# Which PSUM bank pairs w_in's tiles take: the third and the seventh tile, and the order of pairs in the third batch

## The chip, the cores and the metric

The kernel runs on one core of a Trainium2 chip. A core has five engines with queues of their own: TensorE (PE; its weight loads are listed as PEld), VectorE (DVE), ScalarE (ACT), GpSimd (POOL) and SyncE (SP, which issues DMAs). TensorE writes its results to PSUM, which has eight banks here, each of 128 partitions by 512 float32; this kernel uses all eight. The metric is device time in microseconds, the median of several runs.

## What is computed

Cosine attention over 8 batches, 12 heads, 448 rows of 64 elements, followed by a feed-forward layer with an exact GELU:

```python
q_n = q / (np.linalg.norm(q, axis=-1, keepdims=True) + 1e-06)
k_n = k / (np.linalg.norm(k, axis=-1, keepdims=True) + 1e-06)
scores = np.matmul(q_n, k_n.transpose(0, 1, 3, 2)) / tau
attn = np.exp(scores - np.max(scores, axis=-1, keepdims=True))
attn = attn / (np.sum(attn, axis=-1, keepdims=True) + 1e-09)
attn_out = np.matmul(attn, v)                 # (8, 12, 448, 64)
x = attn_out.transpose(0, 2, 1, 3).reshape(3584, 768)
h = x @ w_in                                  # (3584, 2048)
g = 0.5 * h * (1.0 + erf(h / sqrt(2)))
return g @ w_out                              # (3584, 768)
```

## The kernel before

Batches run one after another, b = 0 to 7. The twelve heads of a batch form NQ = 3 groups of four; group g0 = 3b is a batch's first. The order of all instructions is written out by hand, and each engine works through its own in that order, waiting where a result or a buffer is not there yet.

**Attention.** For each group, q and k are loaded (SyncE), squared (GpSimd, L159), reduced (VectorE, L168), turned into inverse norms, scaled to bf16 (GpSimd, L204) and transposed by DMA (L216). Then come seven score passes per group, one for each chunk c of 64 keys for the group's four heads: `scores` (L242) issues four matmuls into a pair of PSUM banks, and `exps` (L252) has ScalarE write exp of both banks to SBUF as bf16. `visit(b, pairs)` (L637) runs the next passes of batch b, one for each number in `pairs`; the number says which bank pair the pass takes. A pass can write its pair only when the exponential of the pair's last pass has been read out. The sums of the exponentials come either from TensorE (`sums`, L311) or, for a batch's third group, from GpSimd (`folded`, L264). `values` (L325) multiplies them with v into a bank pair, too, and `normalise` (L359) has VectorE multiply the result with the inverse sums; that product is two of the six row blocks of x. `weighted(g, p)` is values and normalise of group g in pair p.

**Feed-forward.** `first(b)` multiplies x of batch b with w_in: 16 tiles (m = 0 to 15) of 128 rows of the hidden layer by 448 columns, each six matmuls (L800; KD = 6 row blocks of x), and GELU by ScalarE (L853) into g. The second product, with w_out, is cut into pieces of 16 matmuls (`second_pieces`, L396), which are run as filling between the score passes of the next batch: `run()` takes the next number of them.

**The banks.** Three pairs of two banks, 0, 1 and 2, serve score passes, values and some tiles of w_in. Two single banks, `mm_tile`, alternate between the other tiles of w_in, the sums and the w_out pieces. In `first`, `pairs` (L795) says which tiles take a pair: an entry m: p gives tiles m and m + 1 the two banks of pair p. All other tiles take the single banks in turn. For b of 2 and more, tiles 0 to 5 come first, in the order 0, 2, 3, 4, 5, 1, with the first four row blocks of x each; then the fifth row block of all six, then the sixth; then tiles 6, 7, 8 and so on, each complete. The fifth and sixth row blocks of x are the product of the batch's third group, which is the last thing that VectorE makes of attention.

**What stands around the change.** For b = 3 to 6 the score passes that stand directly ahead of `first(b)` belong to batch b + 1:

```python
visit(b + 1, (1, 2))
weighted(g0 + 2, 0)
visit(b + 1, (1,))
```

Then `first(b)` starts with its tiles. For b = 2 the end of attention is the part that the diff shows, and `visit(b + 1, (1, 2))` and `weighted(g0 + 2, 0)` are its last steps. For b = 7 no passes of a next batch exist, and the last step is `both(g0 + 2, 0)`, sums and values of the third group in pair 0; the last score pass, in pair 2, stands ahead of 22 matmuls with w_out. The next batch's attention starts with filling and then takes pairs 1 and 2 for two passes and pair 0 for values.

Of the kernel before, what the change touches and what calls it, by code (L numbers as in the profile page):

```python
# [16 lines left out]
def kernel(  # L17
# [154 lines left out]
    def logs(n):  # L172
        nq = nq_t.pop(n)
        ln_t[n] = nrm.tile(list(nq.shape), F32, tag="lq", name=f"lq{n}")
        nc.scalar.activation(ln_t[n], nq, AF.Ln, bias=tiny)

    def roots(n):
        ln = ln_t.pop(n)
        sr_t[n] = root2[2 if len(groups[n]) == 2 else n % 2][:, :math.prod(shapes[n])]
        nc.scalar.activation(sr_t[n][:, :, 0], ln.rearrange("p j i s c -> p (j i s c)"), AF.Exp, scale=0.5)  # L180

    def inverses(n):
        sr = sr_t.pop(n)
        shape = [128] + shapes[n]
        se = nrm.tile(shape, F32, tag="se", name=f"se{n}")
        nc.vector.tensor_reduce(se.rearrange("p j i s c -> p (j i s c)"), sr, mybir.AxisListType.X, ALU.add)  # L186
        rn = nrm.tile(shape, F32, tag="rn", name=f"rn{n}")
        nc.vector.reciprocal(rn, se)  # L188
        rn_t[n] = rn
# [42 lines left out]
    def scores(g, banks, p=None):  # L232
        qkT = qkT_t[g]
        if p is None:
            p = st_turn[0]
            st_turn[0] ^= 1
        st = pair(p, f"st{g}_{banks[0][1]}")
        for n, (s, c) in enumerate(banks):
            rows = slice(64 * s, 64 * (s + 1))
            for h in range(2):  # L240
                cols = slice(64 * h, 64 * (h + 1))
                nc.tensor.matmul(st[cols, n, :S], lhsT=qkT[rows, 1, c, cols], rhs=qkT[rows, 0, :, cols],  # L242
                                 start=True, stop=True, tile_position=(64 * s, 64 * h))
        st_t[g, banks[0]] = st

    def exps(g, banks):
        st = st_t.pop((g, banks[0]))
        if g not in all_t:
            all_t[g] = ptp.tile([128, C, 2, S], BF16, tag="pt", name=f"pt{g}")
        (s0, c0), (s1, c1) = banks  # L250
        pt = all_t[g][:, c0] if c0 == c1 else all_t[g][:, c0:c1 + 1, s0]
        nc.scalar.activation(pt, st[:, :, :S], AF.Exp, scale=inv_tau)  # L252
        for n, (s, c) in enumerate(banks):
            pt_t[g, s, c] = pt[:, n]
# [106 lines left out]
    def total(g):  # L361
        sums(g)
        turned(g)
        inverted(g)
        spread(g, 0)
        spread(g, 1)

    def weighted(g, p):
        values(g, p=p)
        for h in range(2):  # L370
            if (g, h) not in rs_t:
                spread(g, h)
            normalise(g, h)

    def both(g, p):
        total(g)
        weighted(g, p)
# [66 lines left out]
    def upto(f, n, last=None):  # L444
        last = {load_qk: NG, load_v: NV, root: len(groups), load_wi: NQ + 1, load_wo: 4}.get(f, NU)
        while done.get(f, 0) < min(n, last):
            done[f] = done.get(f, 0) + 1
            f(done[f] - 1)
# [188 lines left out]
    def visit(b, pairs):  # L637
        for p in pairs:
            n, c = passes[at.get(b, 0)]
            at[b] = at.get(b, 0) + 1  # L640
            scores(b * NQ + n, ((0, c), (1, c)), p)
            exps(b * NQ + n, ((0, c), (1, c)))

    def attention(b, fill):
        fill = list(fill)
        if b == 1:
            parts = iter((20, 13, 14, 17, 16, 16))
        elif b == 2:
            parts = iter((20, 16, 16, 16, 16, 14, 14, 15, 1))
        elif b == B - 1:  # L650
            parts = iter((14, 14, 14, 14, 18, 22))
        elif len(fill) == 128:
            parts = iter((20, 18, 18, 18, 14, 24, 4, 6, 6))
        else:
            parts = iter((14, 12, 12, 12, 14, 16, 4, 6, 6))

        def run(n=None):
            for _ in range(next(parts) if n is None else n):
                fill.pop(0)()

        x_t[b] = xp.tile([128, KD, S], BF16, tag="x", name=f"x{b}")
        g0, u = b * NQ, b * NQ + 1
        run()
        upto(scale, u + 3)
        if b == 2:
            upto(load_qk, g0 + NQ + 3)
        upto(transposes, u + 3)
        if b == 1:
            upto(load_qk, g0 + NQ + 2)
            upto(square, u + 4)  # L670
            visit(b, (0, 1, 2))
            run()
            visit(b, (0, 1, 2))
            run()
            upto(load_qk, g0 + NQ + 3)
            visit(b, (0, 1))
            upto(square, u + 5)
            run()
            visit(b, (0, 1, 2))
            both(g0, 0)  # L680
            upto(load_v, b + 3)
            upto(load_qk, g0 + NQ + 4)
            visit(b, (1, 2))
            upto(reduce, u + 4)
            run()
            visit(b, (1, 2, 0))
            both(g0 + 1, 1)
            visit(b, (2, 0))
            logs(6)
            roots(6)  # L690
            run()
            both(g0 + 2, 2)
            inverses(6)
            done[root] = 7
            return
        upto(scale, u + 4)
        if b == 2:
            upto(load_qk, g0 + NQ + 4)
        upto(transposes, u + 4)
        n = 2 * b + 5  # L700

        def norms():
            if n < len(groups):
                logs(n)
                roots(n)
                inverses(n)
                done[root] = n + 1

        if b == 2:
            visit(b, (0, 1, 2))  # L710
            run()
            upto(load_qk, g0 + NQ + 5)
            upto(square, u + 6)
            visit(b, (0, 1, 2))
            run()
            visit(b, (1, 2))
            total(g0)
            weighted(g0, 0)
            upto(load_v, b + 3)
            visit(b, (1, 2))  # L720
            upto(reduce, u + 5)
            run()
            visit(b, (0, 1, 2))
            folded(g0 + 2, range(2))
            run()
            visit(b, (1, 2))
            total(g0 + 1)
            weighted(g0 + 1, 0)
            visit(b, (1, 2))
            folded(g0 + 2, range(2, C - 1))  # L730
            run()
            upto(reduce, u + 6)
            visit(b, (0,))
            folded(g0 + 2, range(C - 1, C))
            visit(b + 1, (1, 2))
            norms()
            run()
            visit(b + 1, (0, 1, 2))
            run()
            turned_all(g0 + 2)  # L740
            run()
            inverted_all(g0 + 2)
            visit(b + 1, (1, 2))
            weighted(g0 + 2, 0)
        else:
            visit(b, (1, 2))
            weighted(g0, 0)
            visit(b, (1,))
            run()
            upto(load_qk, g0 + NQ + 4)  # L750
            visit(b, (2, 0, 1))
            upto(reduce, u + 5)
            run()
            upto(reduce, u + 6)
            visit(b, (2, 0, 1))
            run()
            upto(load_qk, g0 + NQ + 5)
            visit(b, (2, 0))
            total(g0 + 1)
            if b + 1 < B:  # L760
                folded(g0 + 2, range(4))
            weighted(g0 + 1, 1)
            visit(b, (2, 0))
            if b + 1 < B:
                folded(g0 + 2, range(4, C - 1))
            norms()
            run()
            visit(b, (2,))
            if b + 1 < B:
                folded(g0 + 2, range(C - 1, C))  # L770
                upto(load_v, b + 3)
                visit(b + 1, (0, 1))
                run()
                turned_all(g0 + 2)
                run()
                visit(b + 1, (2, 0))
                run()
                inverted_all(g0 + 2)
                run()
# [3 lines that stand above are left out]
            else:  # L783
                run()
                both(g0 + 2, 0)
        assert not fill, len(fill)

    def first(b):
# [3 lines left out]
        nc.scalar.preload_act_table_set(GELU_SET)  # L792
        u = (b + 1) * NQ + 1
        hps = {}
        pairs = ({0: 1, 2: 0, 6: 1, 8: 0}, {2: 0, 4: 1, 6: 2, 8: 0}, {2: 1, 4: 2})[min(b, 2)]  # L795
        ahead = 6 if b else 5

        def mm(m, kds):
# [134 lines left out]
```

## Time and profile before

| | us |
|---|---|
| median of 3 runs | 409.73 (409.33 to 409.84) |
| the profiled execution | 409.18 |
| its span, first to last instruction | 407.4 |

| engine | busy us | share of the span |
|---|---|---|
| ScalarE | 247.2 | 61% |
| GpSimd | 250.0 | 61% |
| VectorE | 239.1 | 59% |

A line of a group view gives the source line, the engine, the operation, the tile written and those read, the shape and the count, then busy time and the mean of one in ns, then the engine's idle time just before and what ended it:

```text
L800 PE MATMUL hp<-x,wi 128*128 128x448 bf16 x768 | 148.5, 352 | 0.8 <-ACT pt L252 0.6
L853 ACT ACTIVATE g<-hp 128x448 bf16<-128x448 f32 x128 | 64.1, 552 | 76.4 <-PE hp L800 75.9
L252 ACT ACTIVATE pt<-st 128x896 bf16<-128x896 f32 x168 | 143.0, 916 | 54.1 <-PE st L242 53.9
L359 DVE TENSOR_TENSOR x<-o,rs 128x448 bf16<-128x448 f32 x48 | 27.9, 610 | 14.2 <-PE o L325 13.2
```

Matmuls overlap: the mean of 352 ns is the length of one from start to its modelled end, and the next starts before that. A line of the timeline gives start and length in us, engine, line, operation, tiles, shape and count, and in brackets the idle time before it with what ended it; instructions that follow each other without a break are merged into one line.

### The profile page before, as it was taken

The page shows a single profiled execution, that of the slowest core. Times are in us where ns is not written, and L with a number is a line of the kernel's source. Part 1 is how long each engine was busy: PE and PEld are TensorE (multiplying, and loading weights), DVE is VectorE, ACT ScalarE, POOL GpSimd, SP SyncE. Part 2 cuts the span into 40 slices and gives each one's busy share as a digit, 9 for nine tenths or more (in the row PEclk, how much of TensorE's full clock was granted, in tenths as well). Part 3 has the DMA queues.
Part 4 walks back from the last instruction along what each step waited for, and adds up shares of the span by engine and source line. Part 5 has one row for each costly group of instructions (what it writes and reads, how often), then busy time and mean ns, then how long its engine had stood idle before and what let it go on. Part 6 is the DMA issues. An engine that isn't in the chain of part 4 may idle for free.

```text
span 407.4 us, 8074 instructions
## 1 busy us (share of the span) xinstructions
PE 400.3 (98%) x3343; PEld 207.7 (51%) x3343; DVE 239.1 (59%) x438; ACT 247.2 (61%) x360; POOL 250.0 (61%) x160
## 2 busy tenths in 40 slices
PE   7999999999999999999999999999999999999996
PEld 3445545555554555555555555545555455455564
DVE  5787215951477966587656975668655981360021
ACT  6995695577767458655566557855656555724300
POOL 5899606084899983999739994799919940000000
PEclk9999999999999999999999999999999999999999
DMA  8999999745494905577173932769032830130033
GB/s 293 260 257 214 204 230 324 155 117 155 109 263 86 216 5 127 181 142 146 29 221 99 213 73 34 237 114 208 0 89 60 158 55 2 39 79 2 0 79 77
DMA packets 66484, 54.52 MB, mean 134 GB/s; under 512 B 38672, under 2 KB 62352, under 8 KB 66448
## 3 DMA queue, kind: packets, MB, share of 16 engines
q1 hardware_dynamic: 54464, 41.79, 40.0%
q0 software_dynamic: 11600, 11.80, 18.1%
q8 instruction: 26, 0.43, 0.4%
q10 hardware_dynamic: 384, 0.43, 0.4%
q14 instruction: 10, 0.08, 0.1%
HBM read 45.61 MB, written 11.01 MB: 139 GB/s over the span
## 4 chain that ended last, share of the span: by engine, by line
PE 87%; ACT 3%; DMA 3%; DVE 3%; POOL 2%; issue 1%; POOLq 0%
PE op L396 34%; PE hp L800 31%; PE st L242 9%; PE o L325 6%; DMA qkT<-qkb 3%; ACT pt L252 3%; PE sm L311 2%; PE spin L453 2%; POOL qkb L204 1%; PE op L415 1%; PE sm L302 1%; POOL sq L159 1%; PE tp L221 1%; DVE nq L168 1%; DVE tr L333 0%
## 5 line engine op out<-in xcount | busy, mean ns | idle before, releaser
L252 ACT ACTIVATE pt<-st 128x896 bf16<-128x896 f32 x168 | 143.0, 916 | 54.1 <-PE st L242 53.9
L800 PE MATMUL hp<-x,wi 128*128 128x448 bf16 x768 | 148.5, 352 | 0.8 <-ACT pt L252 0.6
L396 PE MATMUL op<-wo,g 128*128 128x384 bf16 x864 | 148.9, 327 | 0.0
L396 PEld LDWEIGHTS <-g 128*128 128x128 bf16 x864 | 81.0, 98 | 64.7 <-issue 14.1
L800 PEld LDWEIGHTS <-wi 128*128 128x128 bf16 x768 | 74.4, 98 | 73.9 <-issue 6.2
L853 ACT ACTIVATE g<-hp 128x448 bf16<-128x448 f32 x128 | 64.1, 552 | 76.4 <-PE hp L800 75.9
L204 POOL TENSOR_TENSOR qkb<-qk,rn 128x896 bf16<-128x896 f32 (+1 forms) x50 | 80.1, 1629 | 29.4 <-DVE rn L188 29.2
L400 DVE COPY ot<-op 128x384 f32<-128x384 f32 x54 | 29.3, 542 | 79.0 <-PE op L396 77.0
L264 POOL TENSOR_TENSOR acc<-acc,pt 128x896 f32<-128x896 f32 (+1 forms) x50 | 73.0, 1460 | 4.2 <-ACT pt L252 0.5
L159 POOL TENSOR_TENSOR sq<-qk 128x1792 f32<-128x1792 f32 (+1 forms) x22 | 66.5, 3038 | 13.7 <-DMA qk<-in_k_dram 13.7
L168 DVE TENSOR_REDUCE nq<-sq 128x28 f32<-128x1792 f32 (+2 forms) x30 | 48.6, 1633 | 10.1 <-POOL sq L159 7.3
L242 PE MATMUL st<-qkT 64*64 64x448 bf16 x672 | 49.5, 358 | 0.7 <-DVE x L359 0.3
L325 PE MATMUL o<-pt,v 64*64 64x448 bf16 x672 | 37.0, 351 | 0.0
L359 DVE TENSOR_TENSOR x<-o,rs 128x448 bf16<-128x448 f32 x48 | 27.9, 610 | 14.2 <-PE o L325 13.2
L264 POOL TENSOR_TENSOR acc<-pt 128x896 f32<-128x896 bf16 (+1 forms) x10 | 14.5, 1453 | 28.6 <-ACT pt L252 28.6
L242 PEld LDWEIGHTS <-qkT 64*64 64x64 bf16 x672 | 16.7, 105 | 24.7 <-issue 17.8
L354 DVE STREAM_TRANSPOSE rs<-rc 128x448 f32<-128x448 f32 x48 | 28.6, 625 | 0.7
L268 DVE TENSOR_REDUCE acc<-pt 128x448 f32<-128x3136 bf16 x5 | 28.1, 5619 | 0.0
L325 PEld LDWEIGHTS <-v 64*64 64x64 bf16 x672 | 18.6, 107 | 14.4 <-issue 4.4
L273 DVE STREAM_TRANSPOSE ta<-acc 128x896 f32<-128x896 f32 x10 | 11.1, 1112 | 17.6 <-POOL acc L264 17.6
L333 DVE STREAM_TRANSPOSE tr<-sm 128x448 f32<-128x448 f32 x14 | 9.1, 648 | 15.1 <-PE sm L311 12.8
L186 DVE TENSOR_REDUCE se<-root 128x28 f32<-128x56 f32 (+2 forms) x18 | 4.0, 221 | 17.9 <-ACT root L180 17.8
(48 smaller groups left out, 170.7 us busy)
## 6 DMA issues: line engine op xcount, KB each, us to landing
qk<-in_q_dram SPq DMA_DIRECT2D x23, 448.0 KB, 5.4
qk<-in_k_dram SPq DMA_DIRECT2D x23, 448.0 KB, 6.0
out_dram<-ot SPq DMA_DIRECT2D x48, 192.0 KB, 3.0
v<-in_v_dram POOLq DMA_DIRECT2D x7, 672.0 KB, 6.8
wo<-in_moe_w_out_dram POOLq DMA_DIRECT2D x4, 768.0 KB, 13.5
wi<-in_moe_w_in_dram POOLq DMA_DIRECT2D x4, 512.0 KB, 14.5
out_dram<-ot SPq DMA_DIRECT2D x12, 96.0 KB, 2.2
wi<-in_moe_w_in_dram POOLq DMA_DIRECT2D x4, 256.0 KB, 13.9
```

What stands on the lines that cost most here:

```text
L159: eng.tensor_tensor(sq[:, part], t[:, part], t[:, part], ALU.mult)
L168: nc.vector.tensor_reduce(nq[:, part], sq[:, part], mybir.AxisListType.X, ALU.add)
L204: eng.tensor_tensor(qkb[:, i, :, s0:s1].rearrange("p c s d -> p s c d"), t[:, i, s0:s1], rn[:, i].to_broadcast([128, s1 - s0, C, D]), ALU. ...
L242: nc.tensor.matmul(st[cols, n, :S], lhsT=qkT[rows, 1, c, cols], rhs=qkT[rows, 0, :, cols], start=True, stop=True, tile_position=(64 * s, 6 ...
L252: nc.scalar.activation(pt, st[:, :, :S], AF.Exp, scale=inv_tau)
L264: nc.gpsimd.tensor_tensor(to, all_t[g][:, 0, s] if c == 1 else to, all_t[g][:, c, s], ALU.add)
L325: nc.tensor.matmul(bank_t[g, h][cols, :S], lhsT=v_t[g][rows, s, c, :], rhs=pt_t[g, s, c][rows], start=(c == 0), stop=(c == C - 1), tile_po ...
L354: nc.vector.transpose(rs, bank_t[g, "rc"][:, h].to_broadcast([128, NB, 32]))
L396: nc.tensor.matmul(ps[:, :NH], lhsT=g_t[sb][:, kf, t * 128:(t + 1) * 128], rhs=wo[:, kf, ni * NH:(ni + 1) * NH], start=(kf == 0), stop=(kf ...
L400: nc.vector.tensor_copy(ot[:, ni * NH:(ni + 1) * NH], ps[:, :NH])
L800: nc.tensor.matmul(hps[m], lhsT=wi[:, kd, m * 128:(m + 1) * 128], rhs=x_t[b][:, kd, :], start=(kd == 0), stop=(kd == KD - 1))
L853: nc.scalar.activation(g_t[sb][:, m, hf * S:(hf + 1) * S], hps.pop(m), AF.Gelu)
```

## The change

It changes which bank pair three things take, and nothing else: the same instructions stand in the same order on each engine, with other PSUM addresses and so other waits.

In `first`, for b = 2 to 7, tiles 2 and 3 move from pair 1 to pair 2, tiles 4 and 5 from pair 2 to pair 1, and tiles 6 and 7 from the two single banks to pair 0. Tile 8 then takes the single bank that tile 0 had, and tile 9 that of tile 1. In the third batch (b = 2) the last passes take the pairs in another order, so that the pass after the second group's values does not take pair 0.

```diff
             run()
             upto(reduce, u + 6)
-            visit(b, (0,))
+            visit(b, (1,))
             folded(g0 + 2, range(C - 1, C))
-            visit(b + 1, (1, 2))
+            visit(b + 1, (2, 0))
             norms()
             run()
-            visit(b + 1, (0, 1, 2))
+            visit(b + 1, (1, 2, 0))
             run()
             turned_all(g0 + 2)
             run()
...
-        pairs = ({0: 1, 2: 0, 6: 1, 8: 0}, {2: 0, 4: 1, 6: 2, 8: 0}, {2: 1, 4: 2})[min(b, 2)]
+        pairs = ({0: 1, 2: 0, 6: 1, 8: 0}, {2: 0, 4: 1, 6: 2, 8: 0}, {2: 2, 4: 1, 6: 0})[min(b, 2)]
```

## The prediction

> **What bounds the kernel now.** I read the page first (busy shares, granted clock), then the waits of TensorE, then the chain of waits through one batch, then the weight loads in order of time. b is the batch number and tile m a 128-row tile of w_in's output, both counted from 0 as in the code: the third tile is tile 2, the seventh tile 6.
>
> From the page, and from the waits of TensorE over the whole span:
>
> ```profile
> PE 400.3 (98%) x3343; PEld 207.7 (51%) x3343; DVE 239.1 (59%) x438; ACT 247.2 (61%) x360; POOL 250.0 (61%) x160
> PEclk9999999999999999999999999999999999999999
> ...
> PE hp L800 <- ACT pt L252: 0.6, 4, 0.2
> PE st L242 <- DVE x L359: 0.3, 1, 0.3
> ```
>
> TensorE is the bound: 98% busy at full clock, the others near 60%. Its waits look tiny, 0.6 us in four places at w_in's matmuls (L800) and 0.3 us in one at the scores (L242), but these idle times are counted from modelled ends of matmuls. So I go by starts. The chain through the end of b = 3's attention (pieces: start, length, what):
>
> ```profile
> 172.08 2.06 PE op L396 x12
> 174.13 0.34 PE st L242 x4
> 174.50 2.63 ACT pt L252 x3
> 177.17 8.48 PE hp L800 x44
> 185.69 9.24 PE hp L800 x48
> ```
>
> The chain leaves TensorE for 2.63 us, for three exponentials in a row, and comes back to the third tile of w_in. The same piece stands at 224.43, 269.16 and 319.09 us (b = 4, 5, 6), and between 124 and 383 us the chain leaves TensorE nowhere else, but for pieces of issue of 0.04 us or less. It holds no DMA and no GpSimd there. Now the weight loads, one ahead of each matmul (start, length, count, and in brackets the idle time before):
>
> ```profile
> 123.37 0.33 PEld L242 LDWEIGHTS <-qkT 64*64 64x64 bf16 x12 [0.66 <-DVE x L359]
> ...
> 126.44 0.33 PEld L242 LDWEIGHTS <-qkT 64*64 64x64 bf16 x12 [0.32 <-issue]
> ...
> 131.66 9.01 PEld L800 LDWEIGHTS <-wi 128*128 128x128 bf16 x49 [0.36 <-issue]
> 140.96 8.80 PEld L800 LDWEIGHTS <-wi 128*128 128x128 bf16 x47 [0.29 <-issue]
> ...
> 176.08 0.68 PEld L800 LDWEIGHTS <-wi 128*128 128x128 bf16 x5 [0.36 <-issue]
> 177.17 8.23 PEld L800 LDWEIGHTS <-wi 128*128 128x128 bf16 x44 [0.41 <-issue]
> 185.69 8.80 PEld L800 LDWEIGHTS <-wi 128*128 128x128 bf16 x47 [0.29 <-issue]
> ```
>
> In an undisturbed run of loads each takes 0.098 us and the step is (8.80 - 0.10)/46 = 0.189 us, so 0.09 us of idle between two is normal. Three holes are larger. (1) After the fifth load, 0.41 us: four matmuls belong to tile 0, the fifth load is ahead for tile 2, and its matmul is held. The hole is in b = 3 to 6 and not in b = 2 or 7, where the 49 loads are one piece. (2) After the 49th load, 0.29 us, in b = 2 to 7 alike: 48 matmuls make eight tiles, and tile 8's first one is held. It starts with the next load, at 140.96, 185.69, 235.62, 280.35, 330.28 and 373.92. (3) Before the scores at 123.37, 0.66 us where 0.32 is usual. What ends them is seen on the other engines (ScalarE's and VectorE's rows in order of time):
>
> ```profile
> 123.24 0.54 DVE L400 COPY ot<-op 128x384 f32<-128x384 f32 x1
> ...
> 130.27 1.73 ACT L252 ACTIVATE pt<-st 128x896 bf16<-128x896 f32 x2 [0.86 <-PE st L242]
> 137.74 3.76 ACT L853 ACTIVATE g<-hp 128x448 bf16<-128x448 f32 x8 [4.44 <-PE hp L800]
> 142.29 0.54 ACT L853 ACTIVATE g<-hp 128x448 bf16<-128x448 f32 x1 [0.79 <-PE hp L800]
> ...
> 177.14 1.28 ACT L792 ACT_TABLE_LOAD   x1
> ...
> 179.28 0.62 DVE L359 TENSOR_TENSOR x<-o,rs 128x448 bf16<-128x448 f32 x1
> ...
> 180.49 0.62 DVE L359 TENSOR_TENSOR x<-o,rs 128x448 bf16<-128x448 f32 x1
> 181.03 5.60 DVE L268 TENSOR_REDUCE acc<-pt 128x448 f32<-128x3136 bf16 x1
> ```
>
> **The change part by part.** No instruction is added or removed; only PSUM banks change, and with them what a tile waits for.
>
> *The third tile, b = 3 to 6.* Score passes end in the order pair 2, values in pair 0, pair 1. Before, tile 2 takes pair 1, the last pass, whose exponential ends as the table load begins, 177.14. After, it takes pair 2, whose exponential ends one pass earlier: the three fill 174.50 to 177.12, some 0.86 us each, so near 176.25. Without a wait tile 2 starts four steps after 176.08, at 176.85, so the wait is gone. Tile 4 now needs the last pass, but stands eight more steps on, at 178.36, 1.2 us after it. Saved: 0.41 - 0.09 = 0.32 by the hole; from the pieces, b = 3 takes 177.17 + 8.23 - 176.08 = 9.32 us for 49 loads and b = 2 takes 9.01, so 0.31. I take 0.31, four times: 1.24 us. Lower bound: the profile's own 0.6 us.
>
> *The seventh and eighth tiles, b = 2 to 7.* Before, tiles 0, 1, 6, 7, 8 ... alternate on two single banks, so tile 8 takes the bank of tile 6 and waits for its GELU. Eight GELUs fill 137.74 to 141.50, and the last, tile 7's, starts when its matmuls end, so tile 6's ends just before 140.96, where tile 8 starts. After, tiles 6 and 7 have pair 0, and tile 8 takes tile 0's bank, free since some 138.3 us. Saved: 0.29 - 0.09 = 0.20 us, six times: 1.20 us. The lower bound is 0, if the hole is the issue that the bracket names. The next use of the single banks, tile 10 after tile 8, has spare: the GELU that starts at 142.29 ends at 142.83 and tile 10 would start two tiles after 140.96, at 143.23, 0.4 us later. Both move together, so nothing is late there. Without this cover all would be given back at tile 10.
>
> *Pair 0 for tile 6.* It held the last values, which VectorE turns into x (L359), ended at 181.11. The last of the six row blocks of x is that same product, and the matmuls with it stand ahead of tile 6, so TensorE has waited already: 0 us. Its next user, the first values of the next batch, comes near 153 us for b = 2; tile 7's GELU ends by 141.5, 11 us before.
>
> *The third batch (b = 2).* The order of pairs changes from 0 | 1, 2 | 0, 1, 2 | 1, 2 to 1 | 2, 0 | 1, 2, 0 | 1, 2. The pass at 123.37 used pair 0 and waited for VectorE's product of the values there, whose chain ends at 123.32. Now it takes pair 1, whose exponential ended two passes back, and pair 0 comes third. It starts 0.66 - 0.32 = 0.34 us earlier, at 123.03; the third pass stands 0.4 us behind (twelve matmuls busy 0.76 us, one 0.35), at 123.43, after 123.32. Saved 0.34 us, lower bound 0. Tile 2 of b = 2 now takes pair 2, the last pass: its exponential ends at 132.00 and the tile starts four steps after 131.66, at 132.42, 0.4 us later. Both move together: 0 us.
>
> *Who must now be earlier.* x of the last head group: after the third tile's wait is gone, its two row blocks are needed at 180.62 and 181.75 (24 and 30 steps after 176.08); VectorE's rows end at 179.90 and 181.11. 0.7 us is left, and GpSimd's sums that feed it start with exponentials, so they move too. GpSimd idles 28.9 us in six places between 120 and 383 us waiting for exponentials, so it keeps up.
>
> The sum: 1.24 + 1.20 + 0.34 = 2.78 us of the profiled execution's 409.18 us (span 407.4), which stands 0.55 us below the median of 409.73. I take it off the median: **406.95 us**. With all lower bounds 0.6 us is saved.
>
> The waits view counts 0.9 us for holes that I put at 1.58. The Trainium skill (Perfetto Trace Analysis, Per-engine timelines, Tensor Engine Instruction) says a matmul's reported end is computed from its size, not observed. By it the waits view can't price these holes, and the starts can; by the waits view alone the sum would be 0.9 us, 408.8.
>
> The clock row is 9 in all slices, so the holes cost no clock here. The Trainium skill (TensorE: Matmul & The Clock Gate, A second HAM failure mode) tells of a kernel whose small PSUM stalls made the clock fall; by that rule closing them would give more than 2.8 us, by the row it doesn't.
>
> **The rivals.**
> *A: the hole at tile 8 is issue, as its bracket says.* For: the name. Against: it is always at the one place where two banks are short, and ScalarE is busy without a break until then. Saved 1.24 + 0.34: 408.15. 8%.
> *B: the time is hidden anyway,* a supplier off TensorE ends batches at the same instant. For: x has only 0.7 us of spare. Against: no DMA or GpSimd piece in the chain after 124 us. 409.7. 4%.
> *C: slower.* Tile 6 waits for pair 0 beyond the product, until VectorE's next instruction, the 5.60 us reduction, has ended (b = 2 to 6). In b = 3 that is 186.63 against a start at 182.90: 3.7 us, five times, less 2.8: 425.4. It decides from 0.56 us a batch. For: only that VectorE works in order. Against: the same product releases the matmuls with x while that reduction runs. 2%.
> *D: a part fails,* such as the third batch's 0.34 us or two of the third tiles: 407.3 to 407.9. 6%.
>
> **How the numbers follow.** The forecast has 80%, with its own range 406.4 to 407.5 from the spread of the runs before. A and D lie up to 408.2, so 406.2 to 408.2 holds well over 8 in 10. All lower bounds at once (409.1) would need three separate causes, and I leave that out. What can be told from no change is 0.2%, 0.8 us. Faster: the forecast, A and D, 94%; same: B, 4%; slower: C, 2%.
>
> **What would show it.** In the profile after: no wait of hp L800 for pt L252; the 2.63 us pieces of ScalarE gone from the chain; 96 loads of L800 in one piece, with no 0.41 or 0.29 before any; 0.32 instead of 0.66 near 123 us. A hole that moves to tile 10, or one at tile 6, would prove me wrong, as would an unchanged 0.29 at tile 8.

## The result, and the profile after

| | before | after |
|---|---|---|
| median us (6 runs each) | 409.78 | 407.03 |
| range | 409.33 to 410.82 | 406.79 to 407.22 |
| profiled execution, its span | 409.18, 407.4 | 407.06, 405.3 |

The ratio is 0.9928, with a 95% interval of 0.9915 to 0.9941: 2.75 us less by the medians, clear of no change. The forecast was 406.95 us (2.78 us less). Here and below, medians and ratios leave out the executions that ran some 6 us longer at a granted clock of 0.976 to 0.984, which several of the kernels had.

The page's busy line and clock row of the changed kernel, and below them the waits of TensorE over the whole span:

```profile
PE 398.9 (98%) x3343; PEld 207.9 (51%) x3343; DVE 239.0 (59%) x438; ACT 247.3 (61%) x360; POOL 250.0 (62%) x160
PEclk9999999999999999999999999999999999999999
...
PE spin L453 <- DVE root L91: 1.9, 1, 1.9
PE st L242 <- DMA qkT<-qkb: 0.6, 1, 0.6
PE st L242 <- ACT pt L252: 0.2, 1, 0.2
```

The busy share is 98% before and after, so it could not have told of this change. The waits of hp L800 for pt L252 and of st L242 for x L359 are gone. What is left is start-up and one wait for a DMA transpose near 59 us, before the first changed instruction.

The chain of waits through the end of b = 3 (start, length, what):

```profile
172.19 2.06 PE op L396 x12
174.25 0.50 PE st L242 x8
174.75 1.32 PE o L325 x28
176.08 0.19 PE st L242 x4
176.27 18.27 PE hp L800 x96
```

The 2.63 us piece of ScalarE is out of the chain, and all 96 matmuls of w_in are one piece. In order of time the weight loads say the same:

```profile
123.68 0.45 PEld L242 LDWEIGHTS <-qkT 64*64 64x64 bf16 x12 [0.32 <-issue]
...
131.97 17.90 PEld L800 LDWEIGHTS <-wi 128*128 128x128 bf16 x96 [0.36 <-issue]
...
176.19 17.90 PEld L800 LDWEIGHTS <-wi 128*128 128x128 bf16 x96 [0.36 <-issue]
```

The brackets of 0.41 and 0.29 us are gone from these two batches and from b = 4 to 7, and the 0.66 near 123 us is the usual 0.32. (These twelve loads take 0.45 and not 0.33 us, because the last four come late: they start at 124.02, just after VectorE's product of the second group ends at 123.96. The four matmuls with them start at 124.08, at their usual distance, so nothing is lost.)

The profiled spans differ by 2.1 us only. The rest was lost before the change begins. The DMA wait near 59 us in the two profiled executions, before and after:

```profile
58.50 0.57 PE L242 MATMUL st<-qkT 64*64 64x448 bf16 x8 [0.26 <-DMA qkT<-qkb]
```

```profile
59.16 0.57 PE L242 MATMUL st<-qkT 64*64 64x448 bf16 x8 [0.62 <-DMA qkT<-qkb]
```

After it this execution of the changed kernel is 0.66 us late: 0.36 us from this wait, and 0.30 us because two more of the warm-up matmuls at its start (L453) ran at 0.37 us a step in place of 0.19. Comparing the start of each matmul with its counterpart, it then gains 0.34 us at the third batch's scores, 0.32 at each of four third tiles and 0.19 to 0.20 at each of six ninth tiles: 0.34 + 4 x 0.32 + 6 x 0.196 = 2.8 us. It gains and loses nothing anywhere else after 60 us.

### The profile page after: what moved, and what is told of

Its sections match the earlier page's. It is cut to its first block, busy times and chain, and to the rows that moved or that the text cites. A ratio compares the mean times of both kernels' runs of the same rounds, so it can differ in the third digit from the quotient of the medians.

```text
span 405.3 us, 8074 instructions
## 1 busy us (share of the span) xinstructions
PE 398.9 (98%) x3343; PEld 207.9 (51%) x3343; DVE 239.0 (59%) x438; ACT 247.3 (61%) x360; POOL 250.0 (62%) x160
## 4 chain that ended last, share of the span: by engine, by line
PE 91%; DMA 3%; POOL 2%; DVE 2%; issue 1%; ACT 0%; POOLq 0%
PE op L396 34%; PE hp L800 32%; PE st L242 10%; PE o L325 8%; DMA qkT<-qkb 3%; PE spin L453 2%; PE sm L311 2%; PE op L415 1%; POOL qkb L204 1%; PE sm L302 1%; POOL sq L159 1%; PE tp L221 1%; DVE nq L168 1%; DVE rn L188 0%; ACT pt L252 0%
## 5 line engine op out<-in xcount | busy, mean ns | idle before, releaser
L252 ACT ACTIVATE pt<-st 128x896 bf16<-128x896 f32 x168 | 143.1, 916 | 54.0 <-PE st L242 53.7
L800 PE MATMUL hp<-x,wi 128*128 128x448 bf16 x768 | 146.9, 353 | 0.0
L800 PEld LDWEIGHTS <-wi 128*128 128x128 bf16 x768 | 74.4, 98 | 71.4 <-issue 2.9
L242 PE MATMUL st<-qkT 64*64 64x448 bf16 x672 | 49.5, 358 | 0.8 <-DMA qkT<-qkb 0.6
L359 DVE TENSOR_TENSOR x<-o,rs 128x448 bf16<-128x448 f32 x48 | 28.0, 610 | 13.7 <-PE o L325 12.7
L242 PEld LDWEIGHTS <-qkT 64*64 64x64 bf16 x672 | 16.8, 105 | 24.7 <-issue 18.1
```

The source lines that it names most:

```text
L800: nc.tensor.matmul(hps[m], lhsT=wi[:, kd, m * 128:(m + 1) * 128], rhs=x_t[b][:, kd, :], start=(kd == 0), stop=(kd == KD - 1))
```

## The experiments

In all of them the pairs are those of b = 2 to 7. The diffs of the first three are against the kernel before, the others against the changed kernel; `...` marks what is left out. For each, "starts" means that the start of each matmul of its profiled execution is compared with that of the same matmul in the kernel named.

**The third tile alone**

```diff
-        pairs = (..., {2: 1, 4: 2})[min(b, 2)]
+        pairs = (..., {2: 2, 4: 1})[min(b, 2)]
```

> Only tiles 2 to 5 change pairs (b = 2 to 7); tiles 6 and 7 stay in the single banks and the third batch keeps its old order of pairs. My theory: the hole after the fifth load of w_in goes in b = 3 to 6 (0.32 us each), the hole after the 49th load (0.20 us, b = 2 to 7) and the 0.66 us ahead of the scores near 123 us stay: 1.27 us less than before, about 408.5 us. Rival (the parts hide each other: an earlier third tile only makes tile 8 wait longer for its GELU): the hole after the 49th load grows by what the first one loses and the time stays at 409.7.

Measured: 408.58 us, ratio 0.9982 (0.9964 to 1.0001); the interval just touches no change, widened by one execution of 412.89 us among twelve, so here the profile decides. Starts against the kernel before: 0.32 us gained at the third tile of b = 3, 4, 5 and 6 and nothing else after 60 us. Its weight loads in b = 3:

```profile
176.42 9.01 PEld L800 LDWEIGHTS <-wi 128*128 128x128 bf16 x49 [0.36 <-issue]
185.72 8.80 PEld L800 LDWEIGHTS <-wi 128*128 128x128 bf16 x47 [0.29 <-issue]
```

The first hole is gone (49 loads in one piece of 9.01 us), the second is still 0.29 us. It did not grow, so the rival falls: the two holes do not hide each other.

**The seventh tile alone**

```diff
-        pairs = (..., {2: 1, 4: 2})[min(b, 2)]
+        pairs = (..., {2: 1, 4: 2, 6: 0})[min(b, 2)]
```

> Only tiles 6 and 7 take pair 0 (b = 2 to 7); tiles 2 to 5 and the third batch are as before. My theory: the hole after the 49th load goes in six batches (0.20 us each), the 0.41 us after the fifth load stays in b = 3 to 6: 1.18 us less than before, about 408.6 us. Rival (that hole is instruction issue, as the bracket in the profile names it): it stays at 0.29 us and the time is 409.7.

Measured: 408.60 us, ratio 0.9974 (0.9961 to 0.9986). Starts against the kernel before: 0.196 to 0.198 us gained in each of six batches. Weight loads in b = 3:

```profile
176.66 0.68 PEld L800 LDWEIGHTS <-wi 128*128 128x128 bf16 x5 [0.36 <-issue]
177.75 17.12 PEld L800 LDWEIGHTS <-wi 128*128 128x128 bf16 x91 [0.41 <-issue]
```

Now it is the other way round: the 0.41 stays, the 0.29 is gone. The bracket called the hole issue; the change of a bank closed it. So it was a wait for the bank, whatever the bracket says. In the kernel before, the GELU of tile 6 in b = 2 and the first matmul of tile 8 stand like this:

```profile
140.31 0.60 ACT L853 ACTIVATE g<-hp 128x448 bf16<-128x448 f32 x1
140.96 0.35 PE L800 MATMUL hp<-x,wi 128*128 128x448 bf16 x1
```

The GELU ends at 140.91, and the matmul starts 0.05 us later.

**The third batch's order alone**

```diff
+            visit(b, (1,))
...
+            visit(b + 1, (2, 0))
...
+            visit(b + 1, (1, 2, 0))
...
         pairs = (..., {2: 1, 4: 2})[min(b, 2)]
```

> Only the order of pairs in the third batch changes. My theory: 0.32 us of idle instead of 0.66 ahead of the scores near 123 us, all other holes as before: 0.34 us less, about 409.4 us, hardly to be told by the median but by the profile. Rival (the pass in pair 0, now third, waits instead): a hole of about 0.3 us between the second and third pass and no gain.

Measured: 409.22 us, ratio 0.9988 (0.9980 to 0.9997). Starts against the kernel before: 0.341 us gained at the first pass after the second group's values, nothing else changes after 60 us. The weight loads of that pass and the two behind it:

```profile
123.20 0.45 PEld L242 LDWEIGHTS <-qkT 64*64 64x64 bf16 x12 [0.32 <-issue]
```

The pass in pair 0, now third, does not delay its matmuls.

**The changed tiles with the old order of the third batch**

```diff
-            visit(b, (1,))
+            visit(b, (0,))
...
-            visit(b + 1, (2, 0))
+            visit(b + 1, (1, 2))
...
-            visit(b + 1, (1, 2, 0))
+            visit(b + 1, (0, 1, 2))
```

> The changed pairs of w_in's tiles with the old order of pairs in the third batch. My theory: 0.66 us of idle is back near 123 us and nothing else: 0.34 us above the changed kernel, about 407.4 us; the order of pairs is not needed for the tiles' gain. Rival (tile 2 in b = 2 now takes the pair of the last pass and needs the new order): a hole after the fifth load of b = 2 and 0.3 us more than that.

Measured: 407.41 us, ratio 0.9956 (0.9933 to 0.9979); one execution of 412.61 us among eleven pulls the ratio up, and by the medians it is 2.3 us less than before. Starts against the changed kernel: 0.341 us lost at that pass, nothing else after 60 us. Its weight loads:

```profile
123.82 0.33 PEld L242 LDWEIGHTS <-qkT 64*64 64x64 bf16 x12 [0.66 <-DVE x L359]
...
132.12 17.90 PEld L800 LDWEIGHTS <-wi 128*128 128x128 bf16 x96 [0.36 <-issue]
```

The 0.66 is back and the 96 loads of b = 2 are whole, so tile 2 does not need the new order. The parts add up: by the medians 1.0 + 1.0 + 0.4 = 2.4 us for the three alone, by starts 1.28 + 1.18 + 0.34 = 2.8. The medians of single parts are no better than a few tenths of a microsecond.

**Pair 0 for tiles 8 and 9 in place of 6 and 7**

```diff
-        pairs = (..., {2: 2, 4: 1, 6: 0})[min(b, 2)]
+        pairs = (..., {2: 2, 4: 1, 8: 0})[min(b, 2)]
```

> As the changed kernel, but pair 0 goes to tiles 8 and 9 in place of 6 and 7. My theory: the hole came from tile 8 waiting for tile 6's GELU, and any bank that spares tile 8 this wait does as well: tiles 6 and 7 take the banks of tiles 0 and 1 and tile 10 that of tile 6, long free. No hole in the 96 loads, time equal to the changed kernel, about 407.0 us. Rival (what helps is that tiles 6 and 7 leave the single banks, so that their start waits for no GELU): a hole of about 0.2 us after the 37th or the 49th load in six batches, 408.2 us.

Measured: 406.71 us, ratio 0.9933 (0.9921 to 0.9944), like the changed kernel. From 60 us on, its starts differ from the changed kernel's by no step. Weight loads in b = 3:

```profile
176.55 17.90 PEld L800 LDWEIGHTS <-wi 128*128 128x128 bf16 x96 [0.36 <-issue]
```

So tiles 6 and 7 can stay in the single banks: it is enough that tile 8 needs another bank than tile 6's.

**Pair 0 for tiles 10 and 11**

```diff
-        pairs = (..., {2: 2, 4: 1, 6: 0})[min(b, 2)]
+        pairs = (..., {2: 2, 4: 1, 10: 0})[min(b, 2)]
```

> As the changed kernel, but pair 0 goes to tiles 10 and 11 in place of 6 and 7. My theory: tile 8 has to wait for tile 6's GELU again, so the 0.29 us hole after the 49th load is back in all six batches, and the time is 1.18 us above the changed kernel, about 408.2 us. Rival (two more banks anywhere in the stage give the slack): no hole, 407.0 us.

Measured: 408.49 us, ratio 0.9969 (0.9956 to 0.9982). Starts against the changed kernel: 0.197 us lost at tile 8 in each of six batches. Weight loads in b = 3:

```profile
177.09 9.01 PEld L800 LDWEIGHTS <-wi 128*128 128x128 bf16 x49 [0.36 <-issue]
186.38 8.80 PEld L800 LDWEIGHTS <-wi 128*128 128x128 bf16 x47 [0.29 <-issue]
```

So two more banks help only if tile 8 is spared tile 6's GELU. These two runs and the seventh tile alone settle what the hole was. The 0.3 us beyond the expected 408.2 is not this hole: in the profiled execution (408.92 us) 0.7 us was lost against the changed kernel in the first 60 us, where the DMA wait took 1.2 us.

**Tile 4 in the pair of the last values**

```diff
-        pairs = (..., {2: 2, 4: 1, 6: 0})[min(b, 2)]
+        pairs = (..., {2: 2, 4: 0, 6: 1})[min(b, 2)]
```

> As the changed kernel, but tiles 4 and 5 take pair 0, that of the last values, and tiles 6 and 7 take pair 1. Now a tile stands on pair 0 before VectorE's product is done. My theory: every wait for a bank ahead of w_in's tiles is paid in full, as no other engine holds a reserve that fills it. From the changed kernel's profile the product ends, plus 0.05 us, later than tile 4's own start by 2.75, 2.81, 0.70, 2.81, 0.70 and 0.81 us for b = 2 to 7: 10.6 us in sum, about 417.6 us, with holes of that size after the 13th load. Rival (the wait is made up later, since GELUs and the next passes are not on the path): less than 3 us in sum, under 410 us. Also open: whether a hole of 2.8 us costs clock, which would show below 1.00 in the stretches after it and give more than 417.6.

Measured: 420.68 us, ratio 1.0273 (1.0256 to 1.0291). Starts against the changed kernel: 2.74, 2.81, 0.69, 2.81, 0.70 and 0.81 us lost at tile 4, 10.56 us, each within 0.02 us of the expected. None is made up later, so the rival falls. But the span is 13.8 us longer, and the rest is clock. Weight loads in b = 2:

```profile
132.03 2.01 PEld L800 LDWEIGHTS <-wi 128*128 128x128 bf16 x12 [0.36 <-issue]
137.06 0.13 PEld L800 LDWEIGHTS <-wi 128*128 128x128 bf16 x2 [3.02 <-DVE x L359]
137.41 0.15 PEld L800 LDWEIGHTS <-wi 128*128 128x128 bf16 x1 [0.22 <-issue]
```

And the busy times by stretch: stretch, its length, then busy time and count for PE, PEld, DVE, ACT and POOL; the third number from the end is the granted clock. The stretches are ahead of b = 2's hole, just after it and later, then just after b = 3's hole and after b = 5's:

```profile
132.00:134.30 2.30, 2.30 (x16) 1.09 (x12) 2.10 (x10) 1.65 (x2) 2.30 (x2) 1.00 0.00 0
137.06:140.00 2.94, 2.94 (x9) 1.20 (x10) 2.94 (x1) 0.00 (x0) 2.94 (x2) 0.51 1.05 240
140.00:143.00 3.00, 3.00 (x17) 1.56 (x16) 3.00 (x2) 0.72 (x2) 2.77 (x4) 1.00 1.12 236
185.50:188.50 3.00, 2.99 (x16) 1.58 (x17) 3.00 (x1) 0.00 (x0) 3.00 (x2) 1.00 1.02 205
282.67:286.50 3.83, 3.83 (x12) 1.62 (x13) 3.83 (x1) 0.00 (x0) 3.83 (x3) 0.58 1.11 232
```

After the holes of b = 2 and b = 5 the clock stands near half for some 3 us (in b = 5 from the fourth matmul after the hole on), and the step from one matmul to the next is 0.37 us in place of 0.19; this costs 1.4 and 1.7 us by the starts. After the equally long hole of b = 3 the steps are the usual ones. 10.56 + 3.1 is 13.7 of the 13.8 us; the other 0.1 arose in the first 60 us.

**Filling the wait that is left**

```diff
-            parts = iter((20, 13, 14, 17, 16, 16))
+            parts = iter((20, 17, 10, 17, 16, 16))
```

> The changed kernel, with four matmuls of w_out moved from after to before the second group of score passes in b = 1. In the changed kernel's profile one wait of TensorE is left that is not start-up: 0.6 us near 59 us, where a score pass waits for a DMA transpose. My theory: the four matmuls (0.65 us) fill that wait, 0.3 to 0.6 us less, about 406.6 us. Rival (the pass that then comes later makes ScalarE's exponentials late, or the DMA's landing moves from run to run by more than that): no difference, 407.0 us.

Measured: 406.54 us, ratio 0.9927 (0.9914 to 0.9939). The DMA wait is gone from its profile. Since the changed kernel had 0.9928 in a run of its own, both were then run side by side.

> The changed kernel itself, beside the next one on the same chip: 407.0 us, and a wait for a DMA transpose near 59 us that differs from run to run (0.3 to 0.6 us so far).

> The changed kernel with four matmuls of w_out moved ahead of the second group of score passes in b = 1, beside the changed kernel on the same chip. My theory: that wait is filled in each run, so it is 0.3 to 0.6 us below the changed kernel. Rival: the start before 50 us varies by as much, and the two can't be told apart (within 0.2 us).

Measured: the changed kernel 406.76 us (ratio 0.9932, 0.9918 to 0.9945), with the fill moved 406.41 us (0.9920, 0.9907 to 0.9934). That is 0.35 us, within overlapping intervals. And the profile does not give it to the fill: in this execution of the changed kernel the DMA wait did not occur at all, and the 0.5 us between the two spans arise in the first 8 us, where the changed kernel had three more of its warm-up matmuls at the slow step of 0.37 us. Score matmuls near 59 us of the changed kernel in this execution, without a bracket:

```profile
58.60 0.81 PE L242 MATMUL st<-qkT 64*64 64x448 bf16 x12
```

Whether moving the fill gains anything is left open. It is the lowest time of the study, but not told from the changed kernel.

## Why the prediction was right

*The sum.* 1.24 + 1.20 + 0.34 was forecast; the starts give 1.28, 1.18 and 0.34, which is 2.80, and the medians 2.75 in all. That the medians meet the forecast within 0.03 us is in part luck: the changed kernel run again gave 2.68 us, and the spans of the two profiled executions 2.1.

*The third tile.* Shown by the run with it alone. It waited for the last pass's exponential, and one pass earlier is early enough.

*The seventh tile.* The lower bound of 0, rival A, rested on the bracket "issue". It is refuted by three runs: the hole closes with pair 0 at tiles 6 or 8 and is back with pair 0 at tile 10. The load of the held matmul stands ahead of the hole (49 loads, 48 matmuls), so the bracket stands at the load behind it. That this load itself waited for no semaphore, and so got the name, is an inference; the cause of the hole is shown.

*The third batch.* 0.341 us in both directions, alone and taken out of the change. The spare was small: the product that pair 0 waits for ended 0.12 us ahead of the third pass, where the forecast had 0.11.

*The covers.* x of the last head group was said to have 0.7 us of spare. VectorE's products in b = 3 after the change:

```profile
179.40 0.62 DVE L359 TENSOR_TENSOR x<-o,rs 128x448 bf16<-128x448 f32 x1
180.61 0.62 DVE L359 TENSOR_TENSOR x<-o,rs 128x448 bf16<-128x448 f32 x1
```

They end at 180.02 and 181.23; the matmuls that read them start 24 and 30 steps after 176.20, at 180.75 and 181.89: 0.7 and 0.6 us later. Pair 0 at tile 6 cost nothing, so rival C falls, and rival B with it, since all that was gained arrived at the end. No part failed, so D, which put a failure of one at 6%, did not come about.

*Waits view or starts.* By the waits view the sum was 0.9 us, by the starts 2.78; the runs gave 2.75. What the Trainium skill says of a matmul's reported end (Perfetto Trace Analysis, Per-engine timelines, Tensor Engine Instruction), that it is computed, fits: the modelled ends covered two thirds of the holes.

*Clock.* The forecast took no clock cost for the small holes, against the account of the Trainium skill (TensorE: Matmul & The Clock Gate, A second HAM failure mode) of PSUM stalls that make the clock fall. The granted clock was 1.00 around them before and after, and the gain was that of the holes alone. What the forecast did not look for is how long a hole may be; see the last section.

## What to carry to other kernels

Where TensorE is 98% busy, look at the starts of its instructions for steps that are longer than their like: here eleven holes of 0.2 to 0.34 us were worth 0.7%, and the waits view priced them at a third. When such a hole repeats at the same tile of each batch, ask which reader of the tile's bank ends last. Here a bank whose reader ended one pass earlier closed the third tile's hole in full, and a spare pair helped only where it spared the waiting tile its wait: at tiles 6 or 8, not at 10. A bank whose reader ends late belongs to a tile that starts later still: pair 0 cost nothing at tile 6 and 10.6 us at tile 4.

## What the runs showed of the hardware that was not expected

A hole of 2.8 us in TensorE's matmuls can cost half the clock for some 3 us after it: granted 0.51 and 0.58 after two of three such holes in one execution, 1.00 after the third. The holes of 0.2 to 0.8 us cost none. How many holes cost clock may differ from one execution to the next: two others of this kernel had the same mean clock of 0.992 and lay within 0.6 us of the profiled one, a fourth had 0.988 and 422.29 us, but none of these three was profiled. The Trainium skill (TensorE: Matmul & The Clock Gate, HAM oscillation) gives some 3.4 us as the gap above which the clock falls. The holes here were shorter (2.9 to 3.0 us from the start of the last matmul ahead to the next), so that figure is not a safe limit.

Why one of the three was spared can be estimated from the same trace. The weight loads around the slow stretch of b = 5 begin and end like this (between the two lines each load stands alone, 0.37 us from the next):

```profile
282.67 0.68 PEld L800 LDWEIGHTS <-wi 128*128 128x128 bf16 x5 [3.09 <-DVE x L359]
...
286.54 3.42 PEld L800 LDWEIGHTS <-wi 128*128 128x128 bf16 x18 [0.22 <-issue]
```

By the lengths of the matmuls' steps, the speed of TensorE changes in this execution at 6.85 us (the end of the slow start), 139.96 (the end of b = 2's slow stretch), 283.33 and 286.74 us (b = 5's). The last two are 3.41 us apart, and all four lie on one grid of 3.413 us: 39, 81 and 82 periods after the first. If the clock is set once in each such period, the hole of b = 5 (279.86 to 282.67) lies almost whole in one period, 2.8 us of it, and that of b = 2 (134.32 to 137.06) has 2.2 us in one that ends at 136.55, still inside the hole, while that of b = 3 (182.71 to 185.51) is cut at 184.34 into 1.6 and 1.2 us. The clock would then fall when somewhere between 1.6 and 2.2 us of a period are idle. This is an estimate from one execution, and no run was made to test it.

The wait for the DMA transpose near 59 us was 0.26 (before), 0.62 (after), 0.70, 0.44, 0.59, 1.28, 1.18 and 0.42 us in eight profiled executions with the same instructions up to there, and absent in two more. That spread, and the opening matmuls at the slow step, make most of the differences between spans that the changed part does not explain.
